# Agent attention and a squared-ReLU layer on one core: small work read a session later, an allowance of it for each engine, and the values' work as four chains

## The chip, the cores and the metric

The kernel runs on one core of a Trainium2 chip. The metric is the device time of one execution in microseconds (us); the median of the runs shown is what two versions are compared by. A change of under 0.2% (some 4 us) is taken as no change.

## The reference, cut to what matters

```python
# q, k, v: (4, 12480, 128); agents: (4, 49, 128); all float32
def sm(a, b):
    s = scale * (a @ b.transpose(0, 2, 1))
    s = s - s.max(-1, keepdims=True)
    e = np.exp(s)
    return e / (e.sum(-1, keepdims=True) + 1e-09)
agent_v = sm(agents, k) @ v            # 49 x 128 for each of 4 batches
x = (sm(q, agents) @ agent_v).reshape(49920, 128)
h = np.maximum(x @ w_in, 0.0)          # w_in 128 x 2048
return h * h @ w_out                   # w_out 2048 x 128
```

## The kernel before, in words

agent_v @ w_in is worked out once for each batch, as a table of 98 rows (high and low halves of 49 agents) by 2048 columns, `aw_hi`, with the rest of the low half in `aw_ex`. A token's hidden layer is then its 49 weights (`w`, and `x` for the rest) times this table.

**Sessions.** The tokens go in 52 blocks of 960 (13 to a batch). A block has 8 sessions, so there are 416, 104 to a batch. Below, session 18 of a batch is its nineteenth, and "session 6 of a block" its seventh. A session of the main work is, on TensorE (PE): eight matmuls into two PSUM tiles `h`, four with `w` (`main`) and four with `x` (`rest`), then twelve matmuls into `o` (`second`) with the results of the session two before. ScalarE (ACT) and VectorE (DVE) do `square` and `divide` for each of the two tiles: ACT `r` = relu(h), DVE `gg` = r*h, ACT `g_hi` = r squared and rounded; then `g_lo` = gg - g_hi, by GpSimd (POOL) in two instructions for the first tile and by DVE for the second, for which gg stays in PSUM in `h`'s place. `h` has three buffers and a session takes two of them. So the second tile of a session can be filled once DVE has made the first tile's `gg` of the session before: that is the loop PE -> ACT r -> DVE gg -> PE.

**Small work.** All else is cut in pieces by generators ("lanes") that yield the letter of the engine whose turn it is: B is a matmul piece that takes the one spare PSUM bank (`psa`), A is ACT, D is DVE, G is POOL (GG is a longer piece), S is the queue of SyncE (SP), which issues every DMA in order. `fill` takes pieces at six places of a session: B between `main` and `rest`; A and D after the first tile's `square` and `divide`; S, G, A and D after the second tile's. `fill(what, most)` goes once through the lanes and lets each move on that has the letter, up to `most` letters. In the steady part every instruction is chained to the one before it on its engine (`queued`), so what this Python order says is the order on each engine; only the part before it is ordered by a scheduler.

- `queries(n)` makes `w` and `x` of block n: scores of the agents (B), maximum and subtraction (D), exponential (ACT, `qe`), sum and reciprocal (DVE, `z`), product (POOL, `qe`), transposition (DVE, `et`), split (POOL, `et_hi`, `et_lo`), and then a chain of DMAs: `et_hi` and `et_lo` to DRAM (`d`), eight reads back to `w`, then `w<-w` and four `x<-w`. It starts `AHEAD` sessions before the block n-1.
- `keys_lane(b)`: the scores of the next batch's 13 key blocks, each a B piece, an ACT copy `s` and a DVE maximum; then `maxima`.
- After the maxima, the values: `halves_lane` splits each of 13 value blocks `vt` into a high and a low half (`vs`), `weights_lane` makes the exponentials (`d`) and their halves (`e2`, shown as `e` in the profile), `sums_lane` multiplies the two (B, `psa<-vs,e`) and adds on DVE (`av`).
- `tables(b)` then makes `aw_hi` and `aw_ex` in four slices, each a B piece (`psa<-win,avT`), an ACT copy (`aw_hi`), a DVE piece (`aw_lo`, two buffers), and five DMAs.

Before the change, the values' two POOL lanes have these steps, and the letters are taken in the same session as far as `most` goes:

```python
def value_halves(vt, vs, out):
    yield "G";  pool.tensor_copy(vs[:, :, :C], vt)
    yield "GG"; pool.tensor_sub(vs[:, :, C + 1 : 2 * C + 1], vt, vs[:, :, :C])
def value_weights(b, i, out):
    yield "G";  pool.tensor_sub(d, st["s"][i], mb)
    yield "A";  act.activation(d, d, AF.Exp, scale=scale)
    yield "GG"; pool.tensor_copy(e[:, :, :NA], d); pool.tensor_sub(e[:, :, NA:], d, e[:, :, :NA])
```

Of the kernel before, what the change touches and what calls it, by code (L numbers as in the profile page):

```python
# [9 lines left out]
F32 = mybir.dt.float32  # L10
# [9 lines left out]
NT = 8  # L20
BLK = TP * NT
G = BLK // 2
# [10 lines left out]
WARM1 = 0  # L33
PRE = 12
EARLY = 4
AHEAD = 1


@with_exitstack
def agent_attention_relu2(ctx: ExitStack, tc: tile.TileContext, qT, kT, v, agT, w_in, w_out, outT):  # L40
    nc = tc.nc
    C, NTOK = outT.shape
    _, B, NA = agT.shape
# [3 lines left out]
    NB = N // BLK  # L47
# [5 lines left out]
    HT = NT // 2  # L53
# [22 lines left out]
    pe, act, dve, pool, sp_ = (Pinned(e) for e in (nc.tensor, nc.scalar, nc.vector, nc.gpsimd, nc.sync))  # L76
# [74 lines left out]
    last = {}  # L151
    free = [0]
    now = [0]
# [17 lines left out]
    def load_values(b, i, pool, name):  # L171
        vt = pool.tile([TP, NT, C], F32, name=name)
        src = v[b, i * BLK : (i + 1) * BLK, :].rearrange("(p t) c -> p t c", p=TP)
        last[nc.sync] = sp_.dma_start(vt, src)
        return vt

    def scores(b, i, kt):
        st = state.setdefault(b, {"s": []})
        yield "B"
        ps = bank()  # L180
        sv = ps[:TP, : NT * NA].rearrange("p (t a) -> p t a", a=NA)
        for t in range(NT):
            pe.matmul(sv[:, t, :], kt[:, t * TP : (t + 1) * TP], ag[:, b, :], start=True, stop=True)
        yield "A"
        s = sp.tile([TP, NT, NA], F32, name="s")
        act.copy(s, sv)
        yield "D"
        if i == 0:
            st["mx"] = small.tile([TP, NT, NA], F32, name="mx")
            dve.tensor_copy(st["mx"], sv)  # L190
        else:
            dve.tensor_max(st["mx"], st["mx"], sv)
        release()
        st["s"].append(s)
# [48 lines left out]
        nc.vector.tensor_copy(x[:NA, C:], pz[:NA, :1])  # L243

    def value_halves(vt, vs, out):
        yield "G"
        pool.tensor_copy(vs[:, :, :C], vt)
        yield "GG"
        last[nc.gpsimd] = pool.tensor_sub(vs[:, :, C + 1 : 2 * C + 1], vt, vs[:, :, :C].bitcast(F32))
        out.append((now[0] + 5, vs))  # L250

    def value_weights(b, i, out):
        st = state[b]
        mb = st["mb"].rearrange("p (o a) -> p o a", o=1).broadcast_to([TP, NT, NA])
        yield "G"
        d = small.tile([TP, NT, NA], F32, name="d", bufs=2)
        pool.tensor_sub(d, st["s"][i], mb)
        yield "A"
        act.activation(d, d, AF.Exp, scale=scale)
        yield "GG"  # L260
        e = small.tile([TP, NT, K2], F32R, name="e2", bufs=2)
        pool.tensor_copy(e[:, :, :NA], d)
        last[nc.gpsimd] = pool.tensor_sub(e[:, :, NA:], d, e[:, :, :NA].bitcast(F32))
        out.append((now[0] + 5, e))
# [64 lines left out]
    def queries(g):  # L329
        b = g // NB  # L330
# [6 lines left out]
        yield "D"  # L337
# [133 lines left out]
    def halves_lane(b, out, used):  # L471
        yield "S"
        vts = [load_values(b, i, kv, "vt") for i in range(2)]
        yield "-"
        for i in range(NB):
            while i - len(used) >= 2:
                yield "-"
            yield from value_halves(vts[i], split[i % 2], out)
            if i + 2 < NB:
                vts.append(load_values(b, i + 2, kv, "vt"))  # L480

    def weights_lane(b, out, used):
        for i in range(NB):
            while i - len(used) >= 2:
                yield "-"
            yield from value_weights(b, i, out)

    def sums_lane(b, weighted, halved, used):
        for i in range(NB):
            while min(len(halved), len(weighted)) <= i or now[0] < max(halved[i][0], weighted[i][0]):  # L490
                yield "-"
            yield from value_sums(b, i, weighted[i][1], halved[i][1])
            used.append(i)
# [4 lines left out]
        yield from then()  # L498

    lanes = {}  # L500

    def start(gen, ahead=False):
        later = dict(lanes) if ahead else {}
        if ahead:
            lanes.clear()
        lanes[gen] = next(gen)
        lanes.update(later)
        return gen

    def fill(what, most):  # L510
        for gen in list(lanes):
            tag = lanes[gen]
            if tag == "-":
                tag = lanes[gen] = next(gen, None)
                if tag is None:
                    del lanes[gen]
                    continue
            if tag == "B":
                if what != "B" or free[0] is None or now[0] < free[0]:
                    continue  # L520
            elif tag[0] != what:
                continue
            if len(tag) > most:
                continue
            most -= len(tag)
            lanes[gen] = next(gen, None)
            if lanes[gen] is None:
                del lanes[gen]
            if most <= 0:
                return  # L530

    def background(b):
        keys = start(keys_lane(b))

        def then():
            yield from maxima(b)
            e, v, used = [], [], []
            ends = [start(gen) for gen in (sums_lane(b, e, v, used), weights_lane(b, e, used), halves_lane(b, v, used))]
# [56 lines left out]
            load_w_out(dec, n)  # L595

    steady[0] = True
    ffn = ctx.enter_context(tc.tile_pool(name="ffn", bufs=4))
    SESSIONS = SLOTS // 2
    for s in range((total + LAG) // 2):  # L600
        k = 2 * s
        more = k < total
        now[0] = 4 * s
        if more:
            g = k // SLOTS
            if k % (NB * SLOTS) == 0 and g // NB + 1 < B:
                background(g // NB + 1)
            for n in range(1, B * NB):
                if s == max(0, (n - 1) * SESSIONS - AHEAD):
                    start(queries(n), True)  # L610
            hs, outs = main(k)
            fill("B", 1)
            rest(k, outs)
            now[0] += 1
            r, gg = square(k, hs[0])
            divide(k, r, gg)
            fill("A", 1)
            fill("D", 1)
# [4 lines left out]
        now[0] += 1  # L623
        if more:
            r, gg = square(k + 1, hs[1])
            divide(k + 1, r, gg)
        write_out()
        fill("S", 3)
        fill("G", 2)
        fill("A", 1)  # L630
        fill("D", 1)


_NAMES = ["qT", "kT", "v", "agT", "w_in", "w_out"]
# [30 lines left out]
```

## Time and profile before

| | us |
|---|---|
| median of 3 runs | 2228.72 (2227.73 to 2228.75) |
| the profiled execution | 2224.96 |
| its span | 2223.2 |
| busy in the span: PE, DVE, ACT, POOL | 2062.5, 1712.3, 1680.9, 1374.1 |
| mean granted PE clock | 0.964 |

The profiled execution lies 1.8 us above its span and 3.8 us below the median. In the profile PEld is PE's loading of weights, which overlaps its matmuls; SPq is SP issuing a DMA. A row of a group ends with the idle time of the engine just before its instructions and with what ended it; a row of the timeline gives start, duration, engine and operation, and in brackets the idle time before it. A row of a table of windows gives the stretch, its length, the busy time of each engine with the number of its instructions, the granted PE clock, and the DMA engines' share and rate.

### The profile page before, as it was taken

Reading aid. Unit: us, or ns where it says so; the run is one execution under the profiler, and the core shown is the slowest. Engines: PE = TensorE matmul, PEld = TensorE weight load, DVE = VectorE, ACT = ScalarE, POOL = GpSimd, SP = SyncE. Lnnn points to the kernel's source line nnn. Section 1 sums busy time; section 2 is a strip of 40 time slices with the busy share of each in tenths; the row PEclk is TensorE's granted clock in tenths of the full one; section 3 lists DMA queues with packets and bytes.
Section 4 is the critical chain, followed back from the end, with each engine's and each line's share of the span. In section 5 each row is a group of like instructions: output and inputs, shape, how many; then the busy total and the mean of one; then the engine's idle time right before and its main releaser. Section 6 shows DMA issues by size and latency. Waiting matters only on the chain. (4 is left out here: it accounts for less than half of the span.)

```text
span 2223.2 us, 30964 instructions
## 1 busy us (share of the span) xinstructions
PE 2062.5 (93%) x10598; PEld 1601.7 (72%) x10598; DVE 1712.3 (77%) x1894; ACT 1680.9 (76%) x1865; POOL 1374.1 (62%) x1235
## 2 busy tenths in 40 slices
PE   9589899999899999998989999999989999999999
PEld 9478677667678776676767877776767777777777
DVE  5658677777787777777868777777778888888887
ACT  3357777877787777777868777777777888888887
POOL 3345677777454577777745467777755656656565
PEclk9689999999999999999989999999999999999999
DMA  9333222222124322222212422222211212221210
GB/s 291 103 91 97 74 85 74 73 75 67 55 78 128 94 78 65 80 85 64 64 63 92 128 71 79 76 75 71 80 57 58 68 62 65 67 68 60 66 52 27
DMA packets 108381, 178.15 MB, mean 80 GB/s; under 512 B 51640, under 2 KB 81656, under 8 KB 108224
## 3 DMA queue, kind: packets, MB, share of 16 engines
q1 hardware_dynamic: 108224, 176.18, 26.1%
q8 instruction: 84, 1.38, 0.3%
q14 instruction: 73, 0.60, 0.1%
HBM read 102.24 MB, written 51.12 MB: 69 GB/s over the span
## 5 line engine op out<-in xcount | busy, mean ns | idle before, releaser
L64 POOL TENSOR_TENSOR g_lo<-gg,g_hi 128x480 fp32r<-128x480 f32 x832 | 998.7, 1222 | 781.4 <-DVE gg L64 535.3
L64 ACT ACTIVATE r<-h 128x960 f32<-128x960 f32 x832 | 800.8, 962 | 325.9 <-PE h L64 313.6
L64 ACT ACTIVATE g_hi<-r 128x960 fp32r<-128x960 f32 x832 | 837.9, 1007 | 47.6 <-PE o L64 4.9
L64 DVE TENSOR_TENSOR gg<-r,h 128x960 f32<-128x960 f32 x416 | 475.2, 1142 | 207.3 <-ACT r L64 206.6
L64 PE MATMUL o<-g_hi,wo_hi 128*128 128x480 f32 x1664 | 553.2, 414 | 0.0
L64 DVE TENSOR_TENSOR h<-r,h 128x960 f32<-128x960 f32 x416 | 481.9, 1158 | 92.5 <-ACT r L64 86.1
L64 PE MATMUL h<-w,aw_hi 128*128 128x480 f32 x1664 | 462.9, 391 | 88.6 <-DVE gg L64 77.4
L64 DVE TENSOR_TENSOR g_lo<-h,g_hi 128x960 fp32r<-128x960 f32 x416 | 481.7, 1158 | 67.3 <-PE o L64 15.3
L64 PE MATMUL o<-g_hi,wo_lo 128*128 128x480 f32 x1664 | 510.4, 388 | 0.0
L64 PE MATMUL o<-g_lo,wo_hi 128*128 128x480 f32 x1664 | 508.2, 387 | 0.0
L64 PEld LDWEIGHTS h<-w,aw_hi 128*128 128x128 f32 x1664 | 304.0, 189 | 181.0 <-DVE gg L64 124.6
L64 PEld LDWEIGHTS o<-g_hi,wo_hi 128*128 128x128 f32 x1664 | 287.7, 193 | 123.5 <-issue 60.9
L64 PEld LDWEIGHTS o<-g_lo,wo_hi 128*128 128x128 f32 x1664 | 321.0, 193 | 53.1
L64 PEld LDWEIGHTS o<-g_hi,wo_lo 128*128 128x128 f32 x1664 | 320.1, 192 | 52.7
L64 PE MATMUL h<-x,aw_ex 19*128 19x480 f32 x1664 | 215.4, 488 | 27.6 <-DMA x<-w 27.6
L64 PEld LDWEIGHTS h<-x,aw_ex 19*128 19x128 f32 x1664 | 84.0, 184 | 143.5 <-issue 105.3
L64 PEld LDWEIGHTS psa<-ag,qt 128*128 128x128 f32 x816 | 107.0, 205 | 26.0 <-DVE aw_lo L64 22.9
L64 PE MATMUL psa<-ag,qt 128*128 128x49 f32 x816 | 104.4, 285 | 21.7 <-DVE aw_lo L64 21.7
L64 ACT ACTIVATE d<-d 120x392 f32<-120x392 f32 x39 | 20.7, 532 | 96.0 <-POOL d L64 96.0
L64 POOL TENSOR_TENSOR vs<-vt,vs 120x1024 fp32r<-120x1024 f32 x39 | 86.4, 2216 | 0.0
L64 DVE COPY ob<-o 128x480 f32<-128x480 f32 x104 | 67.7, 650 | 19.6 <-PE o L64 19.6
L64 PEld LDWEIGHTS psa<-ag,kt 128*120 128x120 f32 x624 | 73.2, 189 | 4.0 <-DVE qe L64 1.2
(113 smaller groups left out, 954.8 us busy)
## 6 DMA issues: line engine op xcount, KB each, us to landing
qt<-in_qT SPq DMA_DIRECT2D x52, 512.0 KB
out_T<-ob SPq DMA_DIRECT2D x104, 240.0 KB
kt<-in_kT SPq DMA_DIRECT2D x39, 480.0 KB
vt<-in_v SPq DMA_DIRECT2D x39, 480.0 KB
x<-w SPq DMA_DIRECT2D x208, 71.2 KB
d<-et_hi SPq DMA_DIRECT2D x52, 240.0 KB
d<-et_lo SPq DMA_DIRECT2D x52, 240.0 KB
w<-d SPq DMA_DIRECT2D x208, 60.0 KB
```

The source lines that it names most:

```text
L64: ins = issue(*args, **kw)
```

## The change

The diff, cut to its core:

```diff
-AHEAD = 1
+AHEAD = 2
+ROOM = {"A": (0.6, 1.0), "D": (1.6, 1.6), "G": (1.8, 2.0), "B": (1, 1), "S": (3, 3)}
+COST = {"A": 0.5, "D": 0.5, "DD": 1.1, "G": 1.0, "GG": 1.6}
...
     def value_halves(vt, vs, out):
-        yield "G"
-        pool.tensor_copy(vs[:, :, :C], vt)
-        yield "GG"
-        last[nc.gpsimd] = pool.tensor_sub(vs[:, :, C + 1 : 2 * C + 1], vt, vs[:, :, :C].bitcast(F32))
+        both = slice(0, HT), slice(HT, NT)
+        for ts, tag in zip(both, ("A", "A!")):
+            yield tag
+            act.copy(vs[:, ts, :C], vt[:, ts, :])
+        for ts, tag in zip(both, ("G", "G!")):
+            yield tag
+            last[nc.gpsimd] = pool.tensor_sub(
+                vs[:, ts, C + 1 : 2 * C + 1], vt[:, ts, :], vs[:, ts, :C].bitcast(F32)
+            )
         out.append((now[0] + 5, vs))
-    def value_weights(b, i, out):
+    def value_exps(b, i, out):
...
         yield "A"
         act.activation(d, d, AF.Exp, scale=scale)
+        out.append((now[0] + 4, d))
+
+    def value_weights(d, out):
         yield "GG"
...
             yield from value_halves(vts[i], split[i % 2], out)
             if i + 2 < NB:
+                yield "S"
                 vts.append(load_values(b, i + 2, kv, "vt"))
...
+    def wait_after(what):
+        if what in "GS":
+            return 4
+        if now[0] % 4 == 2:
+            return 3 if what == "D" else 0
+        return 1
+
+    def go_on(gen, wait):
+        tag = next(gen, None)
+        if tag is None:
+            del lanes[gen]
+        else:
+            lanes[gen] = tag, now[0] + (0 if tag[-1] == "!" else wait)
+
-    def fill(what, most):
+    def fill(what):
...
+            tag, ready = lanes[gen]
+            if tag[0] != what or now[0] < ready:
+                continue
+            cost = COST.get(tag.strip("!"), 1)
+            if room[what] < cost:
+                break
+            if what == "B" and (free[0] is None or now[0] < free[0]):
                 continue
-            most -= len(tag)
...
+            room[what] -= cost
+            go_on(gen, wait_after(what))
+    def more_room():
+        for what, (each, most) in ROOM.items():
+            room[what] = min(room[what] + each, most)
...
     steady[0] = True
+    free[0] = 0
```

`now` counts 4 to a session, its first half at 1 and its second at 2. A lane that has had a piece waits before the next: 4 counts (a session) after a POOL or SP piece, 3 after a DVE piece of the second half, none after an ACT piece of the second half, else 1. Each engine gains the first number of `ROOM` a session (up to the second), and pieces cost as `COST` says. The high halves of the values are copied by ACT in two pieces of 120x512, where POOL copied 120x1024 at once; POOL's subtraction is cut in two likewise. The exponentials have a lane of their own, so four lanes (sums, halves, weights, exponentials) run side by side.

What this does to the order is shown at three places of the second batch. The first is ACT in sessions 34 and 35 of the batch before (138 and 139 of all), and 35 and 36 in the change; `d` are the exponentials, `vs` the halves of a value block, `vt` the block.

```order
L64 ACTIVATE r_7732<-h_7722 128x960
L64 ACTIVATE g_hi_7736<-r_7732 128x960
L64 ACTIVATE r_7754<-h_7723 128x960
L64 ACTIVATE g_hi_7757<-r_7754 128x960
L64 ACTIVATE d_7767<-d_7767 120x392
L64 ACTIVATE r_7780<-h_7770 128x960
L64 ACTIVATE g_hi_7784<-r_7780 128x960
L64 ACTIVATE r_7801<-h_7771 128x960
L64 ACTIVATE g_hi_7804<-r_7801 128x960
```

```order
L66 ACTIVATE r_7815<-h_7805 128x960
L66 ACTIVATE g_hi_7819<-r_7815 128x960
L66 CAST vs0_106<-vt_7550 120x4x128
L66 ACTIVATE r_7837<-h_7806 128x960
L66 ACTIVATE g_hi_7840<-r_7837 128x960
L66 ACTIVATE r_7874<-h_7855 128x960
L66 ACTIVATE g_hi_7878<-r_7874 128x960
L66 ACTIVATE r_7896<-h_7856 128x960
L66 ACTIVATE g_hi_7899<-r_7896 128x960
L66 ACTIVATE d_7853<-d_7853 120x392
```

The exponential still ends a session on ACT, but its input is now POOL's work of the session before, as the second place shows; and ACT has the copies `vs`.

The second place is POOL in the same sessions (138 to 140 before, 138 to 140 in the change); `g_lo` are the main work's two subtractions.

```order
L64 TENSOR_TENSOR g_lo_7738<-gg_7734,g_hi_7736 128x480 x2
L64 TENSOR_TENSOR d_7767<-s_6250,mb_6908 120x392
L64 TENSOR_TENSOR g_lo_7786<-gg_7782,g_hi_7784 128x480 x2
L64 CAST e2_7816<-d_7767 120x8x49
L64 TENSOR_TENSOR e2_7816<-d_7767,e2_7816 120x8x49
L64 TENSOR_TENSOR g_lo_7835<-gg_7831,g_hi_7833 128x480 x2
L64 TENSOR_TENSOR vs1_107<-vt_7423,vs1_107 120x8x128
```

```order
L66 TENSOR_TENSOR g_lo_7772<-gg_7768,g_hi_7770 128x480 x2
L66 CAST e2_7801<-d_7608 120x8x49
L66 TENSOR_TENSOR e2_7801<-d_7608,e2_7801 120x8x49
L66 TENSOR_TENSOR g_lo_7821<-gg_7817,g_hi_7819 128x480 x2
L66 TENSOR_TENSOR vs0_106<-vt_7550,vs0_106 120x4x128
L66 TENSOR_TENSOR d_7853<-s_6276,mb_6979 120x392
L66 TENSOR_TENSOR g_lo_7880<-gg_7876,g_hi_7878 128x480 x2
```

Before, POOL makes `d_7767` behind the session's `g_lo`, and ACT reads it in the same session; in the change `d_7853` stands in session 139 and ACT's use of it at the end of session 140.

The third place is SP's queue at the first two loads of values of the second batch (`vt`, sessions 17 and 18 of the batch); `out_T` is an output, `qt` a load of queries.

```order
L64 DMA qt_6814<-in_qT 128x1024
L64 DMA out_T<-ob_6922 128x480
L64 DMA vt_6932<-in_v 120x1024
L64 DMA vt_6934<-in_v 120x1024
L64 DMA d_6979<-et_hi_6936 128x480
L64 DMA d_6981<-et_lo_6938 128x480
L64 DMA w_6983<-d_6979 32x4x120
```

```order
L66 DMA qt_6787<-in_qT 128x1024
L66 DMA out_T<-ob_6944 128x480
L66 DMA d_7001<-et_hi_6954 128x480
L66 DMA d_7003<-et_lo_6956 128x480
L66 DMA vt_7007<-in_v 120x1024
L66 DMA vt_7009<-in_v 120x1024
L66 DMA w_7005<-d_7001 32x4x120
```

The first loads stand behind the two writes of `et` now, and ACT's first copy of `vt_7007` comes at the end of session 18, the session in which its load is queued.

In the rest of the order: a block's query scores (B) stand in session 6 of the block instead of 7, POOL's `qe` in session 7 instead of 0, and DVE's `et` stays in session 0, so that it reads a product of the session before; `et_hi` and the DMA chain keep their sessions. A value block takes four sessions in the change, and the 13 run from session 18 to 74 (before: to 80). The four slices of the table stand in sessions 79, 82, 85 and 88 (before: 83, 84, 85 and 86). The first query scores of the steady part come in session 0 (before: 1), and SP's load of the queries after them stands ahead of the first two loads of keys, which before were issued ahead of the steady part.

More of the change, by code (lines that the diff above doesn't have):

```diff
@@ L186, in scores @@
         act.copy(s, sv)
-        yield "D"
+        yield "D!"
         if i == 0:
@@ L336, in queries @@
             pe.matmul(sv[:, t, :], qt[:, t, :], ag[:, b, :], start=True, stop=True)
-        yield "D"
+        yield "DD"
         m = qp.tile([P, NT, 1], F32, name="m", bufs=1)
@@ L479, in halves_lane, with exps_lane @@
             if i + 2 < NB:
+                yield "S"
                 vts.append(load_values(b, i + 2, kv, "vt"))
-    def weights_lane(b, out, used):
+    def exps_lane(b, out, used):
         for i in range(NB):
@@ L485, in weights_lane @@
                 yield "-"
-            yield from value_weights(b, i, out)
+            yield from value_exps(b, i, out)
+    def weights_lane(b, exps, out, used):
+        for i in range(NB):
+            while i - len(used) >= 2 or len(exps) <= i or now[0] < exps[i][0]:
+                yield "-"
+            yield from value_weights(exps[i][1], out)
     def sums_lane(b, weighted, halved, used):
@@ L500, in agent_attention_relu2 @@
     lanes = {}
+    room = {"A": 0.0, "D": 0.0, "G": 0.0, "B": 0.0, "S": 0.0}
     def start(gen, ahead=False):
@@ L505, in start @@
             lanes.clear()
-        lanes[gen] = next(gen)
+        lanes[gen] = next(gen), now[0]
         lanes.update(later)
         return gen
-    def fill(what, most):
-        for gen in list(lanes):
[L512 to L521, printed above, removed]
+    def wait_after(what):
[11 more added lines that the diff above has]
+    def fill(what):
+        for gen in list(lanes):
+            if lanes[gen][0] == "-":
+                go_on(gen, 0)
+        for gen in list(lanes):
+            tag, ready = lanes[gen]
+            if tag[0] != what or now[0] < ready:
                 continue
-            if len(tag) > most:
+            cost = COST.get(tag.strip("!"), 1)
+            if room[what] < cost:
+                break
+            if what == "B" and (free[0] is None or now[0] < free[0]):
                 continue
-            most -= len(tag)
[L526 to L530, printed above, removed]
+            room[what] -= cost
[3 more added lines that the diff above has]
+            room[what] = min(room[what] + each, most)
     def background(b):
@@ L536, in then @@
             yield from maxima(b)
-            e, v, used = [], [], []
-            ends = [start(gen) for gen in (sums_lane(b, e, v, used), weights_lane(b, e, used), halves_lane(b, v, used))]
+            d, e, v, used = [], [], [], []
+            ends = [
+                start(gen)
+                for gen in (
+                    sums_lane(b, e, v, used), halves_lane(b, v, used), weights_lane(b, d, e, used), exps_lane(b, d, e),
+                )
+            ]
             yield "-"
@@ L610, in agent_attention_relu2 @@
                     start(queries(n), True)
+            more_room()
             hs, outs = main(k)
-            fill("B", 1)
+            fill("B")
             rest(k, outs)
@@ L616, in agent_attention_relu2 @@
             divide(k, r, gg)
-            fill("A", 1)
-            fill("D", 1)
+            fill("A")
+            fill("D")
         for n in range(2):
@@ L622, in agent_attention_relu2 @@
         copied_out()
-        now[0] += 1
+        now[0] = 4 * s + 2
         if more:
@@ L627, in agent_attention_relu2 @@
         write_out()
[L628 to L631, printed above, removed]
+        fill("S")
+        fill("G")
+        fill("A")
+        fill("D")
 _NAMES = ["qT", "kT", "v", "agT", "w_in", "w_out"]
```

## The prediction

> **What bounds the kernel now.** I read the page first, then the waits of all engines, then windows cut at the starts of sessions, and last the timeline inside the windows that are too long. PE is busy 93% of the span, and the waits that it feels are these:
>
> ```profile
> PE 2062.5 (93%) x10598; PEld 1601.7 (72%) x10598; DVE 1712.3 (77%) x1894; ACT 1680.9 (76%) x1865; POOL 1374.1 (62%) x1235
> PE h L64 <- DVE gg L64: 77.4, 85, 4.4
> PE h L64 <- DMA x<-w: 27.6, 13, 3.0
> ```
>
> The next windows price a session. They hold: four sessions with no small work; three with key scores; one with query scores; one with a value sum. PE has no idle time in them.
>
> ```profile
> 2193.60:2210.00 16.40, 16.40 (x81) 12.45 (x80) 14.04 (x14) 15.34 (x17) 9.61 (x8) 1.00 0.05 17
> 1265.75:1282.97 17.22, 17.22 (x110) 14.88 (x109) 12.13 (x13) 12.71 (x16) 7.12 (x7) 1.00 0.39 123
> 699.12:704.92 5.80, 5.80 (x38) 5.04 (x37) 4.21 (x5) 4.21 (x5) 2.37 (x3) 1.00 0.34 113
> 1610.09:1615.17 5.08, 5.08 (x29) 4.17 (x29) 3.81 (x4) 3.85 (x5) 4.22 (x5) 1.00 0.11 34
> ```
>
> So PE's floor is 16.40 / 4 = 4.10 us a session, and 1.64 more with key scores (17.22 / 3), 1.70 with query scores, 0.98 with a value sum. The clock there is granted in full (1.00), so a PE without gaps isn't slowed. Against this floor stand the stretches of the values' work in the first three batches, then a block of the last batch (nothing but queries beside the main work), three single sessions after the tables' slices, the first four sessions, and session 8.
>
> ```profile
> 214.86:545.20 330.34, 304.12 (x1496) 231.18 (x1495) 250.59 (x269) 249.78 (x274) 240.54 (x214) 0.96 0.25 75
> 760.76:1089.40 328.64, 304.43 (x1514) 232.19 (x1513) 252.17 (x271) 253.68 (x278) 244.65 (x217) 0.97 0.26 76
> 1305.98:1634.38 328.40, 303.88 (x1514) 232.54 (x1513) 251.63 (x269) 252.33 (x276) 243.60 (x217) 0.97 0.26 76
> 1783.18:1819.40 36.22, 35.10 (x177) 26.73 (x176) 30.54 (x33) 31.06 (x34) 21.66 (x20) 1.00 0.20 64
> 570.20:586.70 16.50, 9.27 (x38) 7.72 (x37) 5.74 (x7) 5.59 (x7) 3.35 (x3) 0.69 0.23 69
> 1114.40:1131.90 17.50, 10.10 (x38) 8.36 (x37) 6.23 (x7) 6.09 (x7) 4.15 (x4) 0.61 0.21 66
> 1659.30:1675.60 16.30, 9.21 (x37) 7.65 (x37) 5.61 (x7) 5.52 (x7) 3.31 (x3) 0.69 0.23 70
> 88.10:118.10 30.00, 25.26 (x104) 19.03 (x105) 22.87 (x40) 17.13 (x24) 14.81 (x16) 0.62 0.20 59
> 143.00:159.90 16.90, 10.19 (x36) 7.43 (x37) 4.88 (x7) 4.32 (x5) 1.44 (x2) 0.60 0.21 69
> ```
>
> The second value stretch has 64 sessions (64 x 20 matmuls, 8 x 16 of queries and 13 x 8 of sums make 1512 of its 1514). Its floor is 64 x 4.10 + 8 x 1.70 + 13 x 0.98 = 288.7, so 39.9 us are lost; the third loses 39.7. The first, with 63 sessions, has a floor of 284.6 and loses 45.7. That is 125.3 us in all, the largest thing to be won.
>
> **Part 1: ACT's exponential no longer waits for POOL (a gain).** ACT is idle 96.0 us before 39 exponentials, 2.46 each:
>
> ```profile
> L64 ACT ACTIVATE d<-d 120x392 f32<-120x392 f32 x39 | 20.7, 532 | 96.0 <-POOL d L64 96.0
> 799.92 0.96 POOL L64 TENSOR_TENSOR d<-s,mb 120x392 f32<-120x392 f32 x1
> 800.91 0.53 ACT L64 ACTIVATE d<-d 120x392 f32<-120x392 f32 x1 [2.84 <-POOL d L64]
> 801.35 0.95 ACT L64 ACTIVATE r<-h 128x960 f32<-128x960 f32 x1
> 802.33 1.16 DVE L64 TENSOR_TENSOR gg<-r,h 128x960 f32<-128x960 f32 x1 [1.62 <-ACT r L64]
> 803.54 0.86 PE L64 MATMUL h<-w,aw_hi 128*128 128x480 f32 x2 [2.13 <-DVE gg L64]
> 800.80:808.81 8.01, 5.88 (x22) 3.99 (x20) 5.87 (x6) 7.77 (x9) 5.05 (x6) 0.79 0.19 70
> ```
>
> Read down: POOL ends d at 800.88, ACT has stood 2.84 us, the main work's r and gg are late behind it, and PE stands 2.13 us. That session lasted 8.01 instead of 4.10, since PE's clock was granted at 0.79 behind the gap: a gap costs about twice its length. The Trainium skill (TensorE: Matmul & The Clock Gate, What's actually happening) says that the clock halves only after a whole idle window of about 3.4 us. Here a gap of 2.13 us already had the price, so the trace decides.
>
> In the changed order, POOL's d stands a session ahead of the exponential, and the exponential a session ahead of POOL's split of it. By the rows above POOL is 2 to 3 us behind ACT, and a session is 4.10, so these waits go. Late next could be ACT itself, since it takes over the copies of the values: 78 pieces of 120x512 in place of POOL's 39.
>
> ```profile
> L64 POOL CAST vs<-vt 120x1024 fp32r<-120x1024 f32 x39 | 41.0, 1051 | 4.8 <-DMA vt<-in_v 4.8
> L147 ACT CAST wo_hi<-t 128x256 fp32r<-128x256 f32 x8 | 3.1, 402 | 6.4 <-DVE t L129 6.4
> L64 ACT ACTIVATE g_hi<-r 128x960 fp32r<-128x960 f32 x832 | 837.9, 1007 | 47.6 <-PE o L64 4.9
> 805.14 0.97 ACT L64 ACTIVATE r<-h 128x960 f32<-128x960 f32 x1
> 1765.06 1.03 PE L64 MATMUL h<-w,aw_hi 128*128 128x480 f32 x4
> 1767.71 1.15 DVE L64 TENSOR_TENSOR gg<-r,h 128x960 f32<-128x960 f32 x1
> 1769.17 1.03 PE L64 MATMUL h<-w,aw_hi 128*128 128x480 f32 x4
> ```
>
> Between 256 elements (402 ns) and 960 (1007) a piece of 512 comes to 0.62 us, 48.4 in all (bounds 0.40 and 1.01 each). Without waits ACT does a session's two r and two g_hi in 805.14 - 801.35 = 3.79. Eight sessions with two values then need 8 x 3.79 + 4 x 0.62 + 2 x 0.53 + one query exponential, taken as 0.53, = 34.4, where PE needs 8 x 4.10 + 1.70 + 2 x 0.98 = 36.5. It fits on average. What a session may be late: gg ended at 1768.86, the second tile of the next session is due 0.43 behind 1769.17, so 0.7 us. A session with one piece (3.79 + 0.62) overruns 4.10 by 0.3, two in a row by 0.6. So the copies cost 0 to 48.4, and I take 1.5 a batch, near the lower end, since the pieces stand singly. POOL loses 41.0 us of copies and becomes freer.
>
> **Part 2: the first copy of a batch waits for its load (a new wait).** ACT's first copy stands in the session in which the load is queued, and SP reaches the load only behind the two `et` writes. Queued behind the copy on ACT is the main work, so PE waits too. Nearest is POOL's one such wait, in the first batch:
>
> ```profile
> 220.58 1.79 SPq L64 DMA_DIRECT2D vt<-in_v  x2
> 228.55 1.04 POOL L64 CAST vs<-vt 120x1024 fp32r<-120x1024 f32 x1 [4.78 <-DMA vt<-in_v]
> 234.47:248.62 14.15, 9.78 (x37) 8.09 (x36) 6.35 (x7) 8.18 (x10) 7.22 (x9) 0.64 0.15 51
> ```
>
> The load landed 8.0 us after its issue at most. In the change it is issued about when ACT comes to the copy, so ACT would wait 3 to 8 us. The third row shows the price of PE's longest gap behind an exponential (4.4 in the waits above): 14.15 where 5.80 is the floor, so 8.35. Bounds are 0 (it lands in time) and 11.7 (17.50 - 5.80, the longest stall above). I take 8 a batch, by the middle row. By the skill's rule of Part 1 a gap under 3.4 us would cost itself alone, some 4 us here, and the sum would come out 12 lower.
>
> Parts 1 and 2 together: 125.3 less 3 x (1.5 + 8) = 28.5 gives a gain of 96.8.
>
> **Part 3: the tables' slices three sessions apart (a gain).** The three single sessions above lost 16.50 + 17.50 + 16.30 - 3 x 5.80 = 32.9:
>
> ```profile
> 1122.04 0.74 DVE L64 SCALAR_TENSOR_TENSOR aw_lo<-psa,rl,aw_hi 49x512 fp32r<-49x512 f32 x1 [7.92 <-DMA aw_ex<-aw_lo]
> 1122.83 3.65 PE L64 MATMUL psa<-ag,qt 128*128 128x49 f32 x16 [7.40 <-DVE aw_lo L64]
> ```
>
> The third slice of aw_lo needs the buffer that the first slice's DMAs still read, and PE's query scores need the bank that this DVE piece frees. With three sessions (12.3 us or more) between slices the buffer is free. The slice of session 82 puts its five DMAs between the reads of w and the copy to x, so I leave 1 us a batch: a gain of 30.
>
> **Part 4: the query chain (a gain).** A block of the last batch takes 36.22, with a floor of 8 x 4.10 + 1.70 = 34.5. The 1.7 has two causes, DVE's z pieces just ahead of a gg, and this one:
>
> ```profile
> 1175.30 0.71 DVE L64 STREAM_TRANSPOSE et<-qe 128x512 f32<-128x512 f32 x1 [1.06 <-POOL qe L64]
> 1177.11 0.70 PE L64 MATMUL h<-w,aw_hi 128*128 128x480 f32 x2 [0.78 <-DVE gg L64]
> ```
>
> With POOL's product a session earlier the wait of 1.06 goes, and PE's 0.78 with it, 1.0 with the slower restart; the z pieces stay where they were. It applies to 11 blocks of the last batch and about 7 of the others' blocks that have no other background: 18 us. Bounds are 0 and 31 (all 1.7). The block's first sessions end about 1 us earlier too, so x lands earlier against its need; outside the value stretches some 5 of x's 27.6 us are not session 8's, of which I take 3.
>
> **Part 5: the start (a loss).** Sessions 0 to 3 lost 30.00 - (4.10 + 5.80 + 2 x 5.74) = 8.6 and session 8 lost 16.90 - 5.74 = 11.2, waiting for x. The DMA chain of block 1 keeps its sessions, so the 11.2 stay, plus 1 for the load of queries now ahead of it. The first key loads, no longer issued early, cost 0 to 8.0 (Part 2's landing); I take 2, since PE stands there for other things anyway. A loss of 3.
>
> **The sum:** 96.8 + 30 + 18 + 3 - 3 = 144.8. Against the profiled execution, 2224.96 - 145 = 2080; the median lies 3.8 above that execution, so 2084.
>
> **The rivals.** ACT sets the pace of the values: all 48.4 of copies end on the path, 2132. For it speaks that two copies stand in neighbouring sessions with 0.7 us to spare; against it the 34.4 of 36.5. Chance 0.12.
>
> All is hidden, the first loads too: 24 less, 2060. For it: the loads may land in 4 rather than 8 us. Chance 0.20.
>
> The DMA chain to x becomes the limit, as sessions shorten and it doesn't:
>
> ```profile
> 1832.72 0.32 SPq L64 DMA_DIRECT2D d<-et_hi  x1
> 1858.59 0.48 PE L64 MATMUL h<-x,aw_ex 19*128 19x480 f32 x1 [1.48 <-DMA x<-w]
> ```
>
> It took 25.9 us there. In the change a block has some 32 us from session 1's start to the need, of which the chain starts after 7. If the remaining 46 blocks waited 1.5 each it would be 2153; most chains are shorter than this one. Chance 0.06.
>
> Slower: every copy of a value waits for its load as the first does, 36 more at 8.35, so 300, and 2384. It decides when a load is issued under 8 us ahead of its copy; in the order it stands five sessions (20 us) ahead. Chance 0.03. The change does nothing: the same waits come back with POOL waiting for ACT's exponential, 2229. Chance 0.02.
>
> **How the numbers follow.** My forecast has 0.57. From 2045 (the hidden case, with part of the z stalls gone) to 2135 (ACT's case) 0.85 or so is held. A change under 0.2% can't be told from none. Faster is all but the last two: 0.95; same 0.02; slower 0.03.
>
> **What would show it.** Right: ACT's d waits for POOL under 10 us in all, PE's waits for gg under 35, no wait of DVE's aw_lo for a DMA; ACT has three waits of a copy for vt, 3 to 8 us each; value stretches of 57 sessions of some 268 us (57 x 4.10 + 7 x 1.70 + 13 x 0.98 + 9.5). Wrong: ACT idle before r falls towards zero in the value stretch while PE still waits for gg (ACT's case), more than 13 waits for x, or waits for vt beyond three.

## The result and the profile after

The changed kernel takes 2121.45 us (median of 4 runs, 2119.51 to 2122.98), the kernel before 2228.22 beside it: a ratio of 0.952, 95% interval 0.9505 to 0.9538. That is 107 us less, where 145 were forecast (2084); the time lies in the stated range of 2045 to 2135. The profiled execution took 2119.5, its span 2117.7. First the page after, then its waits and four of its groups of instructions (DVE's transposition of the query weights, `et`, and its piece of a table's slice, `aw_lo`, are the last two).

```profile
span 2117.7 us, 31084 instructions
PE 2024.0 (96%) x10598; PEld 1588.4 (75%) x10598; DVE 1705.1 (81%) x1894; ACT 1716.0 (81%) x1943; POOL 1342.2 (63%) x1235
```

```profile
PE h L66 <- DVE gg L66: 29.4, 49, 3.5
PE h L64 <- DVE x L242: 12.4, 1, 12.4
PE h L66 <- DMA x<-w: 12.0, 11, 2.8
ACT vs L66 <- DMA vt<-in_v: 11.0, 3, 4.2
PE psa L66 <- issue: 9.0, 3, 3.0
```

```profile
L66 ACT ACTIVATE d<-d 120x392 f32<-120x392 f32 x39 | 20.1, 514 | 0.0
L66 ACT CAST vs<-vt 120x512 fp32r<-120x512 f32 x78 | 47.2, 605 | 11.0 <-DMA vt<-in_v 11.0
L66 DVE STREAM_TRANSPOSE et<-qe 128x512 f32<-128x512 f32 x51 | 35.8, 702 | 0.0
L66 DVE SCALAR_TENSOR_TENSOR aw_lo<-psa,rl,aw_hi 49x512 fp32r<-49x512 f32 x12 | 8.7, 725 | 0.0
```

The 39 exponentials, which stood 96.0 us behind POOL, wait for nothing, and PE's waits for gg fell from 77.4 to 29.4. Three copies wait for their load, 11.0 in all. DVE's `et` no longer waits for POOL's product, nor, in the steady part (L66), `aw_lo` for the DMAs of an earlier slice.

Where the time went is best seen in windows that are cut at the same sessions in both kernels, before first. The rows are sessions 0 to 15 of the first batch; then 16 to 79 (values) and 80 to 95 (tables) of the first, second and third; then the last batch. The first number behind the bounds is the length, then come the busy times of PE, PEld, DVE, ACT and POOL, and PE's granted clock.

```profile
88.12:200.17 112.05, 98.91 (x536) 80.98 (x537) 74.92 (x96) 68.05 (x83) 47.68 (x45) 0.84 0.31 95
200.17:535.99 335.82, 309.38 (x1525) 235.11 (x1523) 255.85 (x274) 253.85 (x279) 244.43 (x218) 0.96 0.25 75
535.99:621.67 85.68, 77.95 (x373) 58.90 (x372) 65.11 (x73) 64.84 (x72) 43.30 (x39) 0.94 0.19 59
750.82:1080.18 329.36, 304.21 (x1508) 231.53 (x1507) 253.48 (x272) 253.50 (x278) 244.61 (x218) 0.97 0.26 76
1080.18:1166.88 86.70, 78.76 (x373) 59.49 (x372) 65.23 (x73) 64.86 (x72) 43.27 (x39) 0.92 0.19 58
1294.47:1625.14 330.67, 305.20 (x1508) 233.13 (x1507) 253.54 (x272) 253.44 (x278) 244.47 (x218) 0.97 0.26 76
1625.14:1710.72 85.58, 77.89 (x373) 58.81 (x372) 65.11 (x73) 64.86 (x72) 43.28 (x39) 0.94 0.19 59
1746.96:2210.00 463.04, 449.11 (x2237) 341.46 (x2236) 391.02 (x407) 399.72 (x425) 276.69 (x242) 1.00 0.18 59
```

```profile
93.31:213.08 119.77, 101.41 (x552) 83.84 (x553) 76.80 (x101) 68.85 (x87) 47.50 (x45) 0.84 0.31 97
213.08:514.35 301.27, 294.02 (x1522) 228.59 (x1521) 253.28 (x277) 266.07 (x306) 233.62 (x217) 1.00 0.29 83
514.35:594.96 80.61, 75.94 (x360) 56.70 (x359) 63.27 (x69) 64.07 (x70) 43.29 (x38) 0.96 0.20 62
723.25:1025.29 302.04, 295.45 (x1523) 229.96 (x1521) 253.46 (x277) 266.26 (x306) 233.45 (x217) 0.99 0.28 83
1025.29:1107.21 81.92, 77.21 (x359) 58.07 (x358) 63.25 (x69) 64.06 (x70) 43.28 (x38) 0.94 0.20 61
1233.33:1535.53 302.20, 296.65 (x1522) 230.71 (x1521) 253.35 (x277) 266.05 (x306) 233.44 (x217) 0.99 0.29 83
1535.53:1616.13 80.60, 75.89 (x359) 56.87 (x358) 63.26 (x69) 64.07 (x70) 43.31 (x38) 0.96 0.20 62
1651.39:2104.57 453.18, 447.31 (x2237) 341.37 (x2236) 390.40 (x403) 399.63 (x424) 276.96 (x242) 1.00 0.19 60
```

- The values' windows gained 34.55 + 27.32 + 28.47 = 90.3. PE's clock there rose from 0.96 or 0.97 to 0.99 or 1.00, with the gaps gone.
- The tables' windows gained 5.07 + 4.78 + 4.98 = 14.8.
- The last batch gained 9.9, and sessions 96 to 119 between the rows (129.15, 127.59 and 36.24 before; 128.29, 126.12 and 35.26 after) 3.3.
- The start lost: its first 16 sessions took 7.7 longer (a key score moved in from the next row, where PE did it in 1.6), and the first main matmul came 5.2 later (93.31 against 88.12).

90.3 + 14.8 + 9.9 + 3.3 - 7.7 - 5.2 is 105.4, and the spans differ by 105.5.

Some of PE's work changed rows, too. The first slice of each table (some 0.9, session 79 instead of 83) and the last value sum (1.0, session 80 before) stood in the tables' rows before and stand in the values' rows now. With these and the key score put back, the values gained some 94, the tables some 9, and the start lost some 11.

### The profile page after: what moved, and what is told of

Its sections match the earlier page's. It is cut to its first block, busy times and chain, and to the rows that moved or that the text cites. A ratio compares the mean times of both kernels' runs of the same rounds, so it can differ in the third digit from the quotient of the medians.

```text
span 2117.7 us, 31084 instructions
## 1 busy us (share of the span) xinstructions
PE 2024.0 (96%) x10598; PEld 1588.4 (75%) x10598; DVE 1705.1 (81%) x1894; ACT 1716.0 (81%) x1943; POOL 1342.2 (63%) x1235
## 5 line engine op out<-in xcount | busy, mean ns | idle before, releaser
L66 POOL TENSOR_TENSOR g_lo<-gg,g_hi 128x480 fp32r<-128x480 f32 x832 | 998.9, 1222 | 686.3 <-DVE gg L66 485.5
L66 ACT ACTIVATE r<-h 128x960 f32<-128x960 f32 x832 | 801.1, 963 | 263.2 <-PE h L66 255.3
L66 ACT ACTIVATE g_hi<-r 128x960 fp32r<-128x960 f32 x832 | 838.3, 1008 | 46.3 <-PE o L66 1.2
L66 DVE TENSOR_TENSOR h<-r,h 128x960 f32<-128x960 f32 x416 | 481.8, 1158 | 130.4 <-ACT r L66 127.1
L66 DVE TENSOR_TENSOR gg<-r,h 128x960 f32<-128x960 f32 x416 | 475.5, 1143 | 133.7 <-ACT r L66 130.9
L66 PE MATMUL o<-g_hi,wo_hi 128*128 128x480 f32 x1664 | 547.6, 410 | 0.0
L66 DVE TENSOR_TENSOR g_lo<-h,g_hi 128x960 fp32r<-128x960 f32 x416 | 481.7, 1158 | 58.1 <-PE o L66 6.6
L66 PE MATMUL o<-g_hi,wo_lo 128*128 128x480 f32 x1664 | 503.6, 384 | 0.0
L66 PE MATMUL o<-g_lo,wo_hi 128*128 128x480 f32 x1664 | 502.6, 383 | 0.0
L66 PE MATMUL h<-w,aw_hi 128*128 128x480 f32 x1664 | 448.3, 386 | 34.7 <-DVE gg L66 29.4
L66 PEld LDWEIGHTS h<-w,aw_hi 128*128 128x128 f32 x1664 | 308.6, 189 | 108.6 <-DVE gg L66 53.4
L66 PEld LDWEIGHTS o<-g_hi,wo_hi 128*128 128x128 f32 x1664 | 283.3, 190 | 122.0 <-issue 51.7
L66 PEld LDWEIGHTS o<-g_hi,wo_lo 128*128 128x128 f32 x1664 | 316.2, 190 | 51.9
L66 PEld LDWEIGHTS o<-g_lo,wo_hi 128*128 128x128 f32 x1664 | 315.7, 190 | 51.9
L66 PE MATMUL h<-x,aw_ex 19*128 19x480 f32 x1664 | 212.9, 486 | 12.0 <-DMA x<-w 12.0
L66 PEld LDWEIGHTS h<-x,aw_ex 19*128 19x128 f32 x1664 | 82.9, 183 | 127.2 <-issue 106.3
L66 PEld LDWEIGHTS psa<-ag,qt 128*128 128x128 f32 x816 | 102.5, 198 | 13.1 <-issue 10.2
L66 PE MATMUL psa<-ag,qt 128*128 128x49 f32 x816 | 100.0, 277 | 9.0 <-issue 9.0
L66 POOL TENSOR_TENSOR vs<-vt,vs 120x512 fp32r<-120x512 f32 x78 | 93.8, 1203 | 0.0
L66 DVE COPY ob<-o 128x480 f32<-128x480 f32 x104 | 67.8, 652 | 25.5 <-PE o L66 25.1
L66 PEld LDWEIGHTS psa<-ag,kt 128*120 128x120 f32 x624 | 74.1, 192 | 8.7 <-DVE g_lo L66 5.2
L66 PE MATMUL psa<-ag,kt 128*120 128x49 f32 x624 | 72.7, 271 | 4.7 <-DVE g_lo L66 4.6
```

The lines of the kernel that those rows point to most:

```text
L66: ins = issue(*args, **kw)
```

## The experiments

The changed kernel is called "after" here. A kernel's time is the median of its runs; "after" has 2121.45. The kernel before ran beside each set, and its median was 2225 to 2229.

### The rule of a session later, taken out (e4_same)

```diff
     def wait_after(what):
-        if what in "GS":
-            return 4
-        if now[0] % 4 == 2:
-            return 3 if what == "D" else 0
-        return 1
+        return 0
```

> The rule that small work reads another engine's result a session later is taken out (a piece may run in the next slot as before); the allowances, the copies on ACT and the four chains stay. Theory: the rule carries the largest part of the gain. ACT's exponentials stand in POOL's session again and wait some 2 us each behind POOL's d, PE's main work with them: of the 39 most cost 2 to 3 us, and the query chain's 0.3 to 1 a block comes back: 2190 to 2230. Rival: the gain came from the copies and the allowance, with fewer pieces side by side on POOL; then the waits stay under 1 us each, 2125 to 2150.

Measured: 2236.1, 1.0033 of the kernel before (1.0016 to 1.0049), so 0.3% above it, although the allowances, the copies on ACT and the four chains are still in it. Its waits, its group of exponentials, its second values' window and its last batch:

```profile
PE h L66 <- DVE gg L66: 77.9, 81, 6.1
ACT d L66 <- POOL d L66: 48.4, 21, 2.8
DVE et L66 <- POOL qe L66: 36.2, 44, 1.1
DVE aw_lo L66 <- DMA aw_ex<-aw_lo: 32.2, 5, 10.3
ACT vs L66 <- DMA vt<-in_v: 18.1, 3, 6.3
```

```profile
L66 ACT ACTIVATE d<-d 120x392 f32<-120x392 f32 x39 | 20.5, 525 | 48.4 <-POOL d L66 48.4
```

```profile
756.52:1104.20 347.68, 314.04 (x1528) 239.57 (x1527) 258.51 (x281) 269.70 (x309) 233.47 (x218) 0.94 0.25 73
1760.67:2223.24 462.57, 449.05 (x2237) 340.50 (x2236) 390.32 (x403) 399.85 (x424) 276.79 (x242) 1.00 0.19 59
```

All three old waits are back: exponentials behind POOL's d, DVE's transposition behind POOL's product, aw_lo behind the DMAs of an earlier slice (the rule also keeps the slices apart). PE waits 77.9 us for gg, where it was 77.4 before the change. But only 21 exponentials wait, and a wait that the kernel before did not have on ACT stands beside them: the first copy of each batch waits some 6 us for its load, and its session takes 12.1 to 12.8 us instead of 4.2. So this run does not price the old waits one by one; it shows that without the rule the rest of the change gains nothing. The last batch takes 462.57, as before (463.04), although the queries still begin a session earlier; it is the spacing inside the chain that brought its 9.9, not the earlier start alone.

### The rule alone (e9_rule), POOL's copies (e5_pool), no allowance (e8_room)

For e5_pool the copies return to POOL:

```diff
-        for ts, tag in zip(both, ("A", "A!")):
-            yield tag
-            act.copy(vs[:, ts, :C], vt[:, ts, :])
+        yield "G"
+        pool.tensor_copy(vs[:, :, :C], vt)
...
-ROOM = {"A": (0.6, 1.0), "D": (1.6, 1.6), "G": (1.8, 2.0), "B": (1, 1), "S": (3, 3)}
+ROOM = {"A": (0.6, 1.0), "D": (1.6, 1.6), "G": (2.4, 2.6), "B": (1, 1), "S": (3, 3)}
```

> The values' copies go back to POOL, one piece of 120x1024 a chunk, and POOL's allowance is raised from 1.8 to 2.4 a session (at most 2.6) so that a chunk still takes four sessions; all else is as in the changed kernel. Theory, the copies' place is worth little: on ACT the value blocks lose 0.7 to 0.8 us each, all of it at the queries' z pieces, so the copies there cost nothing; on POOL the small work and the main work come to some 4.2 us of the 4.56 that a session of these blocks lasts, which still fits, and the first copy's wait for its load moves to POOL, where it costs less: 2105 to 2125. Rival, the copies' place carries a large part of the gain: POOL runs late, its d comes later than a session, and the exponentials wait again 1 to 2 us: 2150 to 2200.

For e8_room only the allowances go up:

```diff
-ROOM = {"A": (0.6, 1.0), "D": (1.6, 1.6), "G": (1.8, 2.0), "B": (1, 1), "S": (3, 3)}
+ROOM = {"A": (2.0, 2.0), "D": (3.2, 3.2), "G": (4.0, 4.0), "B": (1, 1), "S": (3, 3)}
```

> The allowances of ACT, DVE and POOL are raised (2.0, 3.2 and 4.0 a session), so that they hardly bind; the rule of a session later, the copies on ACT and the four chains stay. By the order POOL now has up to three small jobs in a session (3.8 us beside 2.4 of main work), and the tables' slices fall where none stands just ahead of query scores. Theory, the allowance matters: POOL is late in those sessions, the exponentials wait 1 to 2 us for d, and the value blocks lose 2 to 5 us instead of 0.8, less 20 for the tables: 2110 to 2150. Rival, the rule of a session later is enough by itself: value blocks stay near 0.8, and only the tables' 20 show: 2100.

e9_rule has both of these edits (with e8_room's allowances), and exponential and split in one chain:

```diff
         act.activation(d, d, AF.Exp, scale=scale)
-        out.append((now[0] + 4, d))
-
-    def value_weights(d, out):
         yield "GG"
...
-                    sums_lane(b, e, v, used), halves_lane(b, v, used), weights_lane(b, d, e, used), exps_lane(b, d, e),
+                    sums_lane(b, e, v, used), halves_lane(b, v, used), weights_lane(b, e, used),
```

> Of the change only the rule that small work reads another engine's result a session later stays (with the queries begun a session earlier): the copies are POOL's again, the exponentials and their split are one chain again, and the allowances are raised so far that they hardly bind. Theory, the rule alone carries the gain: 2100 to 2112, as the tables' slices also fall where none stands just ahead of query scores. Rival, with copies on POOL and no allowance the jobs pile up there (three in a session) and the exponentials wait again: value blocks lose 3 us instead of 0.8, 2150.

Measured: e5_pool 2107.5 (ratio to before 0.9434 to 0.9482), e8_room 2105.0 (0.9422 to 0.9479), e9_rule 2089.3 (0.9347 to 0.9398). Each is faster than "after" (0.9505 to 0.9538), and the rule alone is the fastest of the three. "Alone" means without those three parts of the change: e9_rule keeps the queries' earlier start, POOL's subtraction in two pieces and the order of the start. e5_pool lies where its theory put it. e8_room lies 5 us over its rival's 2100 and under its theory's range; its exponentials wait for POOL again, but 9.8 us in all and 0.9 at most. e9_rule lies 11 us under its theory. Its waits and the first batch's windows of values and tables:

```profile
PE h L66 <- DVE gg L66: 16.7, 40, 1.6
POOL vs L66 <- DMA vt<-in_v: 5.7, 3, 2.3
ACT d L66 <- POOL d L66: 4.1, 4, 1.8
```

```profile
215.29:514.98 299.69, 295.36 (x1527) 229.85 (x1526) 254.46 (x279) 255.85 (x282) 245.44 (x230) 1.00 0.29 84
514.98:587.37 72.39, 71.32 (x356) 54.03 (x354) 61.59 (x66) 62.94 (x68) 43.44 (x38) 1.00 0.22 68
```

Three things make it better than "after". The first copy of a batch still waits for its load, 5.7 in all, but on POOL, with PE's main work not behind it: PE's longest wait for gg is 1.6 instead of 3.5. And without an allowance the values are done sooner, so that the tables' slices fall in sessions 73, 76, 79 and 82, none of them just ahead of query scores: 72.39 where "after" has 80.61 (two slices fewer lie in this window, 2 x 0.9). And its value blocks with two sums take some 36.54, where "after" has 37.23 and the floor is 8 x 4.10 + 1.70 + 2 x 0.98 = 36.46; e5_pool has 37.03 and e8_room 36.92, so neither edit brings this alone, and why it comes was not followed. So neither the copies on ACT nor the allowance nor the fourth chain was needed for the gain. What the fourth chain does alone wasn't run, nor the rule without the earlier start of the queries.

### The three losses that stayed

**The tables (e1_slice).** In "after" the third slice is in session 85, the queries' scores in 86:

```profile
541.30 0.67 ACT L66 ACTIVATE aw_hi<-psa,rl 98x512 fp32r<-98x512 f32 x1
542.20 0.66 DVE L66 COPY ob<-o 128x480 f32<-128x480 f32 x1 [0.23 <-PE o L66]
545.21 0.73 DVE L66 SCALAR_TENSOR_TENSOR aw_lo<-psa,rl,aw_hi 49x512 fp32r<-49x512 f32 x1
546.04 2.04 PE L66 MATMUL psa<-ag,qt 128*128 128x49 f32 x16 [3.02 <-issue]
541.99:553.68 11.69, 8.66 (x37) 6.89 (x36) 6.89 (x8) 6.11 (x7) 4.43 (x4) 0.75 0.28 92
```

aw_lo reads the bank that the scores need, and stands on DVE behind ob and the main work, 3.9 us after ACT's aw_hi; it has no wait of its own. PE stands 3.02 us until it is done, and the session lasts 11.69 instead of 5.80.

```diff
             cs = slice(n * 512, (n + 1) * 512)
+            while steady[0] and now[0] // 4 % 8 in (3, 4, 5):
+                yield "-"
             yield "B"
```

> The tables' third and fourth slices are kept out of the sessions just ahead of a block's query scores (they come 5 and 8 sessions behind the second instead of 3 and 6); nothing else moves. Theory, the bank: in the changed kernel the third slice stands one session ahead of the query scores, DVE's aw_lo piece frees the bank late, PE waits 3.0 us and its clock drops; sessions 86, 190 and 294 lose 5.9, 7.5 and 6.3 us, 19.7 in all, and these go: about 2102 us. Rival, the buffer: what PE waits for is still the slice's DMAs reading aw_lo, as in the kernel before; then the loss follows the slices to the new place and the time stays at 2119 to 2122.

Measured: 2103.7. The tables' windows are 74.76, 74.49 and 74.31 instead of 80.61, 81.92 and 80.60: 19.6 less, with three slices in them as before. It was the bank.

**The first value load (e2_vt).** Rows of "after" in the second batch, and the session that holds the wait:

```profile
736.99 0.86 SPq L66 DMA_DIRECT2D vt<-in_v  x2
742.80 0.62 ACT L66 CAST vs<-vt 120x512 fp32r<-120x512 f32 x1 [4.24 <-DMA vt<-in_v]
745.60 1.06 PE L66 MATMUL h<-w,aw_hi 128*128 128x480 f32 x2 [3.52 <-DVE gg L66]
741.52:750.91 9.39, 5.87 (x22) 3.92 (x21) 4.60 (x4) 7.96 (x10) 3.95 (x4) 0.82 0.32 77
```

```diff
         def then():
+            vts = []
+            start(loads_lane(b, vts))
+            yield "-"
             yield from maxima(b)
...
-        yield "S"
-        vts = [load_values(b, i, kv, "vt") for i in range(2)]
-        yield "-"
+        while not vts:
+            yield "-"
```

> The first two value loads of a batch are queued when the keys are done, ahead of the maxima, instead of behind them; the copies stay where they are. Theory: ACT's first copy of a batch waits for the load because that is queued in the copy's own session; sessions 18 to 21 of a batch lose about 5, 6.4 and 6.7 us to it. With the load some two sessions (8 us) ahead the three waits of a copy for vt (11.0 us) go, and 15 to 18 us with them: about 2104. Rival: the load only lands later because other DMAs stand ahead of it, or PE waits there for the maxima as well: 2113 to 2121.

Measured: 2107.2. No copy waits for vt any more, and session 20 of the three batches, which lost 3.1, 5.3 and 5.7, has its 4.10: 14.1 in all.

**The start (e3_kt).**

```diff
     def keys_lane(b):
-        yield "S"
+        if b > 1:
+            yield "S"
         kts = [load_keys(b, i, kv, "kt") for i in range(2)]
```

> In the second batch alone the first two key loads are put into the queue ahead of the first block's queries, where the kernel before had them. Theory: what the start lost against the kernel before (the first main matmul 5.2 us later, sessions 0 to 7 6.1 us more) comes from the key loads that stand behind the second query load, and so behind the tables' DMAs: about 10 us go, 2111. Rival, the order of the start: the 5.2 us come from DVE's decoding of the last weights, which now stands ahead of the copy to x; then only the 6 go, 2115. Third: the key loads then compete with the chain to x, and session 8 waits longer: 2121.

Measured: 2112.0 (ratio 0.9435 to 0.9491). The profiled executions differ by 7.0: 3.1 come from the first main matmul (90.17 instead of 93.31) and 1.4 from sessions 0 to 15. The rest is differences of both signs in rows that this edit leaves alone, the largest in the second tables (2.9 less). The copy to x ahead of the tables, in "after", then in e3_kt:

```profile
85.41 0.28 DVE L242 COPY x<-h 49x128 f32<-49x128 f32 x1
```

```profile
75.09 0.28 DVE L242 COPY x<-h 49x128 f32<-49x128 f32 x1
```

The kernel before has it at 73.08. So the place of two key loads also moved the decoding of the last weights ahead of this copy, which put the copy off by 10 to 12 us, of which PE felt 3 to 5, since in e3_kt it waits 6.9 for the tables' DMAs instead. The theory and its rival each hold in part, with smaller amounts.

### z without its addition (e6_z)

What is left in nearly every block of "after" is this, in the last batch:

```profile
1792.21 0.55 DVE L66 TENSOR_REDUCE z<-qe 128x8 f32<-128x392 f32 x1
1793.12 1.11 DVE L66 TENSOR_TENSOR gg<-r,h 128x960 f32<-128x960 f32 x1
1794.29 0.70 PE L66 MATMUL h<-w,aw_hi 128*128 128x480 f32 x2 [0.34 <-DVE gg L66]
```

```diff
         dve.reduce_sum(z, e, axis=AX.X)
-        dve.tensor_scalar_add(z, z, 1e-9)
         dve.reciprocal(z, z)
```

> The addition of 1e-9 to the queries' sums z is left out (the sums are at least 1, so that a float's value doesn't change); DVE's group of three z pieces ahead of a gg becomes two, 0.92 us less 0.17. Theory: of the 0.7 to 0.8 us that each block still loses, all stands behind this group (PE waits 0.34 for gg, and restarts slower), so about half of it goes in some 45 blocks: 10 to 18 us, 2103 to 2111. Rival: gg is late for another reason (ACT's r), and nothing changes: 2119 to 2123.

Measured: 2115.1, a ratio of 0.9487 to 0.9524, which overlaps that of "after". By the profile a block of the last batch loses 0.5 instead of 0.7, the number of PE's waits for gg falls from 49 to 32, and the blocks with values keep their 0.8. But that execution, the slowest of its four, has the same span as that of "after", 2117.7, since other rows lost what these gained. A small gain is likely, about half of what was expected, and not settled by the times.

### Put together (e7_all), and the start once more (e10_late, e11_late_room, e12_split)

e7_all has the four edits of e1, e2, e3 and e6.

> The four edits that take out one loss each, together: slices away from the session ahead of the queries, value loads ahead of the maxima, first key loads ahead of the queries in the second batch, z without its addition. Theory, the losses are separate: 2121.5 less 17.7, 14.3 and 9.5 (measured one by one) and less 10 to 18 for z: about 2066. Rival, they share a cover or the chain to x becomes the limit in shorter blocks: 2075 to 2095.

Measured: 2077.8 (ratio 0.9318 to 0.9349). By its profile the tables gave 19.7, the value loads 14.1, the first main matmul 4.1 and z 3.7, 41.6 of the 42.2 between the spans. The time lies in the rival's range, but not for the rival's reason: the losses are separate, and the forecast of 2066 had z and the key loads too high.

e10_late delays the second batch's key work, in place of e3's edit:

```diff
     def keys_lane(b):
+        while b == 1 and now[0] < 4 * 6:
+            yield "-"
         yield "S"
```

> As the kernel with the four edits together, but in the second batch the key work (loads and scores) begins in session 6 instead of 0, in place of the earlier key loads. Theory: the first block's 16 us and session 8's 11.7 come from key loads that share the DMA queues with block 1's chain to x, and from scores that wait for them; block 0 then has 4.10 a session, the chain (write of et to x landed, some 24 us in an undisturbed block) ends within 3 us of its need, and 15 to 22 us go: 2056 to 2063. Rival: the chain is bound by its start in session 3; shorter sessions then only move the wait to session 8: 2070 to 2080.

e11_late_room has e8_room's allowances as well:

> The kernel of the run before with the raised allowances (2.0, 3.2 and 4.0). Theory: without allowances the value blocks lost 0.5 instead of 0.8, so 18 blocks bring 3 to 6 us. Rival: the same as without, within 2 us.

e12_split is e7_all with a delay of the second batch's scores alone; the first two keys are loaded early, as there:

```diff
     def keys_lane(b):
-        yield "S"
+        if b > 1:
+            yield "S"
         kts = [load_keys(b, i, kv, "kt") for i in range(2)]
         yield "-"
+        while b == 1 and now[0] < 4 * 6:
+            yield "-"
```

> As the run that begins the second batch's key work in session 6, but its first two key loads are queued ahead of the start again; only the scores wait. Theory: there session 8's 11.7 us at x were gone and 23.3 us were lost in session 7 instead, where the key loads queued behind block 1's chain; with two loads in the buffers beforehand the 23.3 fall to 0 to 6 (the third load comes a session after): 2084 less 17 to 23, 2061 to 2067. Rival: the third key load, behind the chain, takes the wait over in session 9: 2072 to 2082.

Measured: e10_late 2084.0, e11_late_room 2097.0, e12_split 2074.3 (ratio 0.9290 to 0.9332), the lowest median here. e10_late's new wait:

```profile
PE psa L66 <- DMA kt<-in_kT: 19.5, 1, 19.5
```

Session 8 lost nothing there, but only because session 7 lost 23.3 to the key load queued behind block 1's chain to x. With the keys loaded early (e12_split) session 7 loses 1.9 and session 8 again 10.7. So the rival of e10_late was right in kind, though 2084.0 lies above both its ranges: that chain is bound by its start in session 3, and shorter sessions ahead of it only move the wait. e12_split lies in its rival's range, but no wait came in session 9, as that rival had it; what its theory overlooked is session 8. Its median is 3.4 under that of e7_all, and their intervals overlap. e11_late_room missed both its theories: with values whose first copy stands in session 25 of the first batch the missing allowance cost 13 us, 12 of them in that first batch (its block 9, counted from 0, takes 43.2 instead of 36.6). In that block 0.9 is a slice that moved in, and session 78 took 9.94 instead of 5.82, by the order of its rows for the bank once more: PE's query scores stood 2.33 us until 512.29, and DVE had read the bank for `rl`, a piece ahead of the first slice, until 512.19. The rest wasn't followed. The edits of e7_all on top of e9_rule were not run.

## Why the prediction was right, and where it was off

The direction, the largest term and its mechanism were right. Each term of the sum against its windows:

| term | forecast | measured, by rows | with moved work put back |
|---|---|---|---|
| Parts 1 and 2, values | 96.8 | 90.3 | 94.2 |
| Part 3, tables | 30 | 14.8 | 9.3 |
| Part 4, query chain and x | 21 | 13.2 | 13.2 |
| Part 5, start | -3 | -12.9 | -11.3 |
| sum | 144.8 | 105.4 | 105.4 |

**Part 1** held: no exponential waits, and e4_same and e9_rule show that the rule does it. The copies on ACT cost little: with them back on POOL (e5_pool, where POOL's allowance rises too) a value block takes 37.03 instead of 37.23, which comes to some 1.5 a batch, as taken.

**Part 2** held in kind: three waits, 11.0 together, forecast 3 to 8 each. They cost 3.1, 5.3 and 5.7, not 8 each. Sessions 18 to 74 took 268.9, 269.7 and 269.9, where the prediction had some 268. That is closer than its terms were, and so partly luck: the loads cost 14.1 where 24 were taken, and the 28.5 left nothing for the z pieces, which Part 4 named and this sum forgot (21 blocks that lose some 0.75 are 16 us, in which the copies' 0.2 a block may be held).

**Part 3** is the step that was mis-sized most. It looked at one resource of a slice, the aw_lo buffer, and with three sessions between slices that wait is indeed gone. But the forecast's own row said that PE waits for a bank, and the bank is freed by DVE, 3.9 us behind ACT's aw_hi. The order put a slice just ahead of the query scores, and that was not checked: sessions 86, 190 and 294 lost 5.9, 7.5 and 6.3, so that 19.7 of the 32.9 stayed, and e1_slice took these away. Like for like the tables gave 9.3 of the 30.

**Part 4**: the wait for POOL's product is gone. Its price of 1.0 a block was nearly right in the last batch (9.9, where 11 were taken); the 7 blocks of other batches gave 3.3. The 3 for x can't be told apart in it: PE's waits for x fell from 27.6 to 12.0, but 14.3 of that lay in the values' windows (15.9 before, 1.6 after), and session 8's loss stayed at 11.2.

**Part 5**: the key loads were priced by their landing alone. Moved behind the second query load they stood behind all of the tables' DMAs, were issued at 104.9 instead of 48.0, and the start's other work was reordered around them. Bounds of 0 and 8.0 for this edit were too narrow. The first key scores of "after":

```profile
109.30 3.41 PE L66 MATMUL psa<-ag,kt 128*120 128x49 f32 x16 [4.58 <-DVE g_lo L66]
```

PE stood 4.58 ahead of them (2.15 in e3_kt), and at a granted clock of 0.50 they took 3.41 instead of 1.6. Of the 12.9, e3_kt gave back 4.6, and 3.4 are these scores themselves; some 5 were not traced.

**Price of a gap.** The forecast put a gap at about twice its length, by two rows. The sessions of the three late loads show that it isn't so regular; that of the second batch is shown under e2_vt, and those of the first and the third are these:

```profile
231.28:238.46 7.18, 4.38 (x21) 2.99 (x20) 3.67 (x4) 6.43 (x9) 3.56 (x3) 1.00 0.42 91
1251.53:1261.36 9.83, 7.22 (x22) 5.01 (x21) 5.76 (x5) 9.01 (x11) 5.27 (x5) 0.65 0.31 71
```

PE stood 2.80, 3.52 and 2.61 us, the granted clock was 1.00, 0.82 and 0.65, and the sessions lost 3.1, 5.3 and 5.7. Ahead of the query scores 3.02 us made a session 5.9 longer (clock 0.75). So the price lay between 1.1 and 2.2 times the gap and did not go by its length; what decides it stays open. The Trainium skill (TensorE: Matmul & The Clock Gate, What's actually happening) has the clock halve only after an idle window of some 3.4 us; behind the gaps of 2.61 and 3.02 it was down as well, so here the measurement decides. By that rule the prediction estimated some 4 us for each load, and for this term that was nearer to the 4.7 measured on average than its own 8; the whole sum by that rule, 12 lower, was further off.

**The rivals.** ACT's pace did not set the end (a value block loses 0.75 of some 37), and waits for vt stayed at three. The time came near the 2132 of ACT's case by other causes; that it lies in the range is partly luck, since no case held Parts 3 and 5 as they came, and in the values two errors cancelled.

## What to carry to other kernels

In a hand-ordered pipeline, leaving a session between an engine's result and the small work on another engine that reads it was worth the whole gain here, with the queries begun a session earlier to make room for it; moving copies to another engine, rationing, and a chain of their own for the exponentials were not needed. When such an order is changed, follow every resource of each moved step (its bank, its buffer, its load, what its queue then holds up), and look at what stands in the session behind it. An edit that gains a little per block can still lose it at the start, where one queue holds loads, tables and weights.

## What was not expected

The wait of a batch's first copy for its load was cheaper on POOL, whose main work is needed later. On ACT (in "after") three waits, 11.0 us in all and 4.2 at most, cost their sessions 14.1; on POOL (in e9_rule) three waits, 5.7 in all and 2.3 at most, left no gap of PE over 1.6, and session 21 behind them took 5.47, 4.53 and 5.10, where e2_vt, without the wait, has 4.26, 4.26 and 4.23: 2.4 in all. The waits differ in length, so the comparison is a rough one. It also needs the session between: in the kernel before, POOL stood 4.78 us for a load and then worked without a break until it had made the next `d` (236.70); ACT's exponential stood 4.82 us behind that, and PE 4.38, its longest wait for gg there.
